# The first loads of a fused attention and SwiGLU kernel put on one DMA queue, with one dummy product fewer

## The chip, the cores and the metric

The kernel runs on one core of one Trainium2 chip. The metric is device time in microseconds (us), the median over several executions. With one core there is no other die to compare with; all runs quoted are of the state "fast". Different experiments ran on different chips, and each was timed in turn with the kernel before on its own chip. "Span" is the length of one profiled execution; it is about 1.7 us shorter than the device time of the same execution.

Engines in the profile: PE is the matrix engine (TensorE), PEld its weight loads, DVE the vector engine, ACT the scalar engine, POOL GpSimd, SP the sync engine, which here only issues loads and stores. SPq and ACTq are the sequencers of SP and ACT issuing a DMA. Queue q1 in the DMA view is the sync queue, q10 the scalar queue.

## The reference

The block mixes linear attention and a SwiGLU over the same x (2048 tokens of 512 values), with a gate per token:

```python
qkv = x @ wqkv                       # 32 heads of 16
phi = lambda t: where(t > 0, t + 1, exp(t)) + 1e-6
kv  = sum over tokens of phi(k) v;   z = sum over tokens of phi(k)
a   = (phi(q) @ kv) / (phi(q) . z + 1e-6) @ wo
b   = (silu(x @ w1) * (x @ w3)) @ w2
out = sigmoid(x . gate_w) * a + (1 - that) * b
```

All inputs are bf16. For this change only the start matters: k needs x transposed and wk, and phi(k) then multiplies x (the products called XP).

## The kernel before

Four loads of 256 KB come first. x tiles 0-1, wk's second half and x tiles 2-3 go by the sync queue, wk's first half by the scalar queue. Behind them on the sync queue come the remaining x tiles, once through a transposing load and once plainly.

```python
dq = nc.sync
dq.dma_start(out=x_sb[:, 0:2, :], in_=x_pairs[0])                       # x tiles 0-1
nc.scalar.dma_start(out=wk_sb[:, 0:2, :], in_=wqkv_r[:, 0:2, D:2*D])    # wk, first half
dq.dma_start(out=wk_sb[:, 2:4, :], in_=wqkv_r[:, 2:4, D:2*D])           # wk, second half
dq.dma_start(out=x_sb[:, 2:TPB, :], in_=x_pairs[1])                     # x tiles 2-3
...                                  # ACT: a one-element exp, which loads its table
for tb in range(1, NTB):
    dq.dma_start(out=xT[...], in_=x2d[...], transpose=True)
    dq.dma_start(out=x_sb[...], in_=x_r[...])
...                                  # all other weights
```

While these loads run PE has nothing to compute. It is given dummy products on constants, meant to have its clock up when work comes (in this trace dummies of 512 columns start 0.42 us apart, products of the same width from 5.5 us on 0.216):

```python
emit_warm(TB, TB, TB, TB, TB, TB, P, P, P)     # six of 512 columns, three of 128
...
emit_xT(0); emit_xT(1)               # PE transposes x tiles 0-1 (xTp), copies by DVE and ACT
for kc, t in ((0,0),(1,0),(0,1),(1,1),(2,0),(3,0)):
    emit_k_mm(k0[t], t, kc)          # kc 0-1 need wk's first half, kc 2-3 the second
emit_k_phi(k0[0], 0)
emit_xT(2); emit_xT(3)               # needs x tiles 2-3
...                                  # ten more key products, then XP and the rest
```

PE's order is fixed by hand, so a product that waits holds back the products behind it.

## Time and profile before

| | before |
|---|---|
| time, median of the first 3 runs | 180.62 us (180.34 to 180.81) |
| span of the profiled execution | 178.7 us |
| PE busy | 174.9 us, 98% |
| PE's first real instruction (xTp) | 3.91 us |
| first product XP | 8.93 us |

The page's first part says what bounds the kernel. Columns: engine, busy us, share of the span, instructions.

```profile
span 178.7 us, 2488 instructions
PE 174.9 (98%) x893; PEld 84.6 (47%) x893; DVE 118.2 (66%) x205; ACT 66.6 (37%) x126; POOL 61.4 (34%) x69
```

The chain of waits in the first 16 us (start, length, what) shows PE alone from 0.84 us on: dummies, transposes, key products, XP, with hardly a gap. (Where two groups of products overlap in the pipeline the chain lets the second start where the first ends, so its XP stands at 9.09; the timeline has the true start, 8.93.)

```profile
0.84 3.04 PE warm L161 x9
3.88 0.03 issue
3.91 1.03 PE xTp L174 x8
4.95 1.54 PE k L184 x6
6.48 0.45 PE xTp L174 x8
6.93 2.16 PE k L184 x10
9.09 0.86 PE XP L204 x4
```

The DMA view lists issues with KB and the time from issue to landing, here in three narrow windows: the issues at 0.80 (scalar) and 0.81 (sync), then wk's second half at 1.26, then x tiles 2-3 at 1.72.

```profile
wk_sb<-in_A_wqkv_dram ACTq DMA_DIRECT2D x1, 256.0 KB, 3.8
x_sb<-in_A_x_dram SPq DMA_DIRECT2D x1, 256.0 KB, 3.1
...
wk_sb<-in_A_wqkv_dram SPq DMA_DIRECT2D x1, 256.0 KB, 4.0
...
x_sb<-in_A_x_dram SPq DMA_DIRECT2D x1, 256.0 KB, 4.3
```

Adding issue and landing: x tiles 0-1 at 3.9, wk's halves at 4.6 and 5.3, x tiles 2-3 at 6.0 us. Each comes 0.04 to 0.63 us before PE uses it (3.91, 4.74, 5.89, 6.32). So the start is balanced closely, and PE waits for none of the last three.

### The profile page before, as it was taken

The numbers are of one execution on the slowest core, as the hardware profiler recorded it, in microseconds if no ns is written. First come the engines' busy times: TensorE is split into PE (matmuls) and PEld (weight loads), VectorE is DVE, ScalarE is ACT, GpSimd is POOL, SyncE is SP. The second block draws the span as 40 slices with busy tenths as digits, with TensorE's granted clock in tenths as the row PEclk, the third lists the DMA queues.
The fourth block names the chain that finished last, engine by engine and source line by source line (L and its number), as shares of the span: only waits on it lengthen the run. The fifth ranks groups of instructions, "written<-read, shape, count | busy, mean of one in ns | idle before, by whom it ended". The sixth has DMA issues, their size and how long they took to land.

```text
span 178.7 us, 2488 instructions
## 1 busy us (share of the span) xinstructions
PE 174.9 (98%) x893; PEld 84.6 (47%) x893; DVE 118.2 (66%) x205; ACT 66.6 (37%) x126; POOL 61.4 (34%) x69
## 2 busy tenths in 40 slices
PE   8999999999999999999999999999999999999993
PEld 3544444474444545444444544444545444444463
DVE  0588867696998837398786375978754669776000
ACT  3642322666533333342433333342433323341221
POOL 5187575646353323262003232620032328100000
PEclk9999999999999999999999999999999999999999
DMA  6999999601005010124000111240001023300011
GB/s 177 265 280 290 298 362 355 216 0 28 9 11 108 0 48 29 44 54 93 0 4 6 38 37 37 59 93 2 0 7 58 15 62 64 61 0 0 29 44 50
DMA packets 29085, 14.88 MB, mean 83 GB/s; under 512 B 19632, under 2 KB 28816, under 8 KB 29072
## 3 DMA queue, kind: packets, MB, share of 16 engines
q1 hardware_dynamic: 28800, 14.46, 29.5%
q10 hardware_dynamic: 272, 0.26, 0.5%
q8 instruction: 7, 0.11, 0.3%
q14 instruction: 6, 0.05, 0.1%
HBM read 8.42 MB, written 2.10 MB: 59 GB/s over the span
## 4 chain that ended last, share of the span: by engine, by line
PE 98%; DVE 0%; issue 0%; DVEq 0%
PE o_ps L355 19%; PE up_ps L318 19%; PE gate_ps L310 19%; PE XP L204 8%; PE o_ps L346 8%; PE q_ps L217 8%; PE k_ps L184 6%; PE r_ps L241 3%; PE k L184 2%; PE o_ps L350 2%; PE warm L161 2%; PE xTp L174 1%; PE kvT_ps L413 1%; PE W_ps L440 0%; DVE o_out L364 0%; PE z_ps L431 0%
## 5 line engine op out<-in xcount | busy, mean ns | idle before, releaser
L318 PE MATMUL up_ps<-xT,w_sb 128*128 128x512 bf16 x160 | 41.1, 379 | 0.0
L310 PE MATMUL gate_ps<-xT,w_sb 128*128 128x512 bf16 x160 | 41.1, 379 | 0.0
L225 POOL TENSOR_TENSOR qz<-pq,z_sb 128x512 f32<-128x512 bf16 x16 | 18.5, 1164 | 60.3 <-DVE pq L145 58.4
L323 ACT ACTIVATE th<-gate_ps 128x512 bf16<-128x512 f32 x40 | 23.9, 597 | 38.1 <-PE gate_ps L310 37.7
L355 PE MATMUL o_ps<-w_sb,hT 128*128 128x512 bf16 (+2 forms) x180 | 37.5, 355 | 0.0
L325 DVE SCALAR_TENSOR_TENSOR gs<-th,gate_ps 128x512 bf16<-128x512 bf16 x40 | 27.4, 684 | 5.8 <-ACT th L323 5.5
L328 DVE TENSOR_TENSOR hT<-up_ps,gs 128x512 bf16<-128x512 f32 x40 | 27.6, 691 | 3.8
L142 DVE TENSOR_SCALAR phi_m<-phi_e 128x512 bf16<-128x512 bf16 x32 | 14.1, 440 | 19.8 <-ACT phi_e L140 19.7
L355 PEld LDWEIGHTS <-hT 128*128 128x128 bf16 x180 | 16.8, 98 | 17.9
L318 PEld LDWEIGHTS <-w_sb 128*128 128x128 bf16 x160 | 15.6, 98 | 18.9
L310 PEld LDWEIGHTS <-w_sb 128*128 128x128 bf16 x160 | 15.6, 98 | 18.7
L360 ACT ACTIVATE o_out<-o_ps,omg 128x512 bf16<-128x512 f32 (+2 forms) x17 | 11.2, 656 | 30.4 <-PE o_ps L355 30.4
L290 POOL TENSOR_TENSOR pqn<-pq,rden 128x512 bf16<-128x512 bf16 x16 | 16.6, 1056 | 14.0 <-DVE rden L283 11.7
L194 POOL TENSOR_TENSOR pks<-pks,pk_sb 128x512 f32<-128x512 f32 x15 | 17.3, 1155 | 8.3 <-DVE pk_sb L145 7.8
L228 DVE TENSOR_REDUCE den<-qz 128x32 f32<-128x512 f32 x16 | 11.0, 685 | 9.0 <-POOL qz L225 8.9
L346 PE MATMUL o_ps<-W_sb,pqT 128*128 128x512 bf16 (+2 forms) x72 | 16.8, 355 | 0.0
L217 PE MATMUL q_ps<-wq_sb,xT 128*128 128x512 bf16 x64 | 16.3, 379 | 0.0
L204 PE MATMUL XP<-pk_sb,x_sb 128*128 128x512 bf16 x64 | 16.2, 379 | 0.0
L140 ACT ACTIVATE phi_e<-k_ps 128x512 bf16<-128x512 f32 x12 | 7.2, 597 | 15.4 <-PE k_ps L184 13.1
L184 PE MATMUL k_ps<-wk_sb,xT 128*128 128x512 bf16 x48 | 12.3, 379 | 0.0
L140 ACT ACTIVATE phi_e<-q_ps 128x512 bf16<-128x512 f32 x16 | 9.6, 597 | 7.0 <-PE q_ps L217 5.8
L145 DVE SCALAR_TENSOR_TENSOR pq<-q_ps,phi_m 128x512 bf16<-128x512 f32 x16 | 11.1, 691 | 0.5
(59 smaller groups left out, 119.3 us busy)
## 6 DMA issues: line engine op xcount, KB each, us to landing
w_sb<-in_B_w_dram SPq DMA_DIRECT2D x6, 640.0 KB, 8.6
out_dram<-o_out SPq DMA_DIRECT2D x15, 128.0 KB, 1.7
x_sb<-in_A_x_dram SPq DMA_DIRECT2D x3, 512.0 KB, 4.0
x_sb<-in_A_x_dram SPq DMA_DIRECT2D x2, 256.0 KB, 3.7
wq_sb<-in_A_wqkv_dram SPq DMA_DIRECT2D x1, 512.0 KB, 5.1
wv_sb<-in_A_wqkv_dram SPq DMA_DIRECT2D x1, 512.0 KB, 6.8
wo_sb<-in_A_wo_dram SPq DMA_DIRECT2D x1, 512.0 KB, 10.0
wk_sb<-in_A_wqkv_dram ACTq DMA_DIRECT2D x1, 256.0 KB, 3.8
```

The costliest lines, as they stand in the source:

```text
L184: nc.tensor.matmul(k_ps[:], lhsT=xT[:, kc, t * P : (t + 1) * P], rhs=wk_sb[:, kc, :], start=(kc == 0), stop=(kc == KC - 1),)
L194: nc.gpsimd.tensor_add(pks[:], pks[:], pk_sb[:, t, :])
L204: nc.tensor.matmul(XP_ps[dc][:], lhsT=x_sb[:, t, dc * P : (dc + 1) * P], rhs=pk_sb[:, t, :], start=(t == 0), stop=(t == NT - 1),)
L217: nc.tensor.matmul(q_ps[:], lhsT=xT[:, kc, ts_tok], rhs=wq_sb[:, kc, :], start=(kc == 0), stop=(kc == KC - 1),)
L225: nc.gpsimd.tensor_tensor(out=qz[:], in0=st[tb, "pq"][:, tt, :], in1=z_sb[:], op=ALU.mult)
L310: nc.tensor.matmul(gate_ps[:], lhsT=w1_sb[:, kc, fsl], rhs=xT[:, kc, tok_sl], start=(kc == 0), stop=(kc == KC - 1),)
L318: nc.tensor.matmul(up_ps[:], lhsT=w3_sb[:, kc, fsl], rhs=xT[:, kc, tok_sl], start=(kc == 0), stop=(kc == KC - 1),)
L323: nc.scalar.activation(out=th[:], in_=gate_ps[:], func=ACT.Tanh, scale=0.5)
L325: nc.vector.scalar_tensor_tensor(out=gs[:], in0=th[:], scalar=1.0, in1=gate_ps[:], op0=ALU.add, op1=ALU.mult)
L328: nc.vector.tensor_tensor(out=st[tb, "hT"][:, fc, :], in0=up_ps[:], in1=gs[:], op=ALU.mult)
L346: nc.tensor.matmul(o_ps[:], lhsT=st[tb, "pqT"][:, c, tsl], rhs=W_sb[:, c, a:b], start=(c == 0), stop=False,)
L355: nc.tensor.matmul(o_ps[:], lhsT=st[tb, "hT"][:, fc, tsl], rhs=w2_sb[:, fc, a:b], start=False, stop=(fc == FC - 1),)
```

## The change

The intent: x tiles 0-1 should not share the DMA engines with wk's first half (in the kernel before, from 2.8 to 3.0 us, 26 packets of the one ran beside 20 of the other), so that they land sooner; then one dummy product can go, and PE begins real work about 0.43 us earlier. The whole diff:

```diff
     dq.dma_start(out=x_sb[:, 0:2, :], in_=x_pairs[0])
-    nc.scalar.dma_start(out=wk_sb[:, 0:2, :], in_=wqkv_r[:, 0:2, D : 2 * D])
+    dq.dma_start(out=wk_sb[:, 0:2, :], in_=wqkv_r[:, 0:2, D : 2 * D])
     dq.dma_start(out=wk_sb[:, 2:4, :], in_=wqkv_r[:, 2:4, D : 2 * D])
     dq.dma_start(out=x_sb[:, 2:TPB, :], in_=x_pairs[1])
@@
-    emit_warm(TB, TB, TB, TB, TB, TB, P, P, P)
+    emit_warm(TB, TB, TB, TB, TB, P, P, P)
```

## The prediction

> **What bounds it now.** TensorE. The page gives PE 174.9 us of a 178.7 us span (98%), and the chain of waits is PE in 98% of it. So time can only be won before the first product that counts, or after the last. At the start the chain reads: issue to 0.84 us; nine dummy products (warm) 0.84 to 3.88; the transposes of x tiles 0-1 (xTp) from 3.91; then key products. From 3.91 on PE is hardly idle. The list of waits shows one stop that a load causes: xTp's weight loads wait 0.3 us for DMA x_sb, issued at 0.81 and landed 3.1 us later, at about 3.9. So dummies and first x load end together; neither is worth shortening alone.
>
> **The load.** In narrow windows of the DMA view the first x load's packets (sync queue) start near 1.75 us. Packets of wk's first half (scalar queue) appear from 2.6 us on, when about 70 of x's 128 packets have run, and take a third to a half of the engines until x is through, near 3.3. [...] With wk behind x on one queue, x's last 60 packets should run at about the 369 GB/s that both got together: 0.33 us instead of 0.7. x then lands near 3.45 (estimate), 0.45 earlier.
>
> **The cost.** One more issue on SP, about 0.45 us, so wk's second half, x tiles 2-3 and the transposing loads are issued that much later. wk's first half landed at 4.6, its first product began at 4.74; wk's second half 5.26, first product 5.89; x tiles 2-3 6.0, transposes 6.32. The engines are saturated from 2.6 us on and the order of bytes hardly changes, so I expect these landings to stay or come slightly earlier. The first transposing load should land near 8.1 and is used at 9.8.
>
> **The dummies.** Cold 512-column products start 0.42 us apart (six from 0.84 to 2.93); hot ones 0.216 us. Dropping one lets PE reach the transposes at about 3.3, x at 3.45: xTp starts about 0.43 us earlier.
>
> **How much is kept.** The hot spacing begins at about 5.1 us[...]. So 0.43 us more of useful work is done at half speed, worth about 0.22 us hot. Small waits for copies in this stretch (0.28 us for a DVE copy) move with it, so some of the rest may be kept. Gain 0.2 to 0.35 us of 180.6, near the spread of the three runs (180.34 to 180.81).
>
> **Predicted: 180.35 us**, 8 in 10 between 180.0 and 180.7. Faster by over 2%: 0.005; within 2%: 0.99; slower by over 2%: 0.005.
>
> **What would show it.** Eight dummies ending near 3.45; first x load landing in about 2.6 us; xTp starting at 3.45 to 3.5; first key product near 4.3; the first product XP (before at 8.93) near 8.65, everything after shifted alike; no new PE wait for wk_sb or x_sb over 0.1 us.
>
> **What would make it wrong.** wk's first half lands later than 4.3 and the first key product waits; x tiles 2-3 land later than 6.0 and their transposes wait; x's landing does not move (PE idles where the dummy was, gain nil); or the clock turns hot later.

180.6 less the gain of 0.2 to 0.35 gives 180.25 to 180.4 us, and 180.35 was named. The 0.22 us is the estimate from this trace, 0.43 us at 0.42 us per product against 0.216; that the start of the hot spacing would stay where it was, on which it rests, was assumed and not shown.

## The result and the profile after

| | before | after |
|---|---|---|
| time, median of 6 runs | 180.47 us (180.28 to 180.81) | 181.43 us (181.08 to 181.53) |
| ratio | | 1.0049, 95% interval 1.0036 to 1.0062 |
| span | 178.7 us | 179.7 us |
| first product XP | 8.93 us | 9.78 us |

A ratio here is the mean time of one kernel's fast runs over that of the other's of the same rounds, so it is not quite the ratio of the medians. The changed kernel is 0.5% slower; it was forecast 0.1 to 0.2% faster, and 181.43 lies outside the range of 180.0 to 180.7. It is within the 2% called "same".

The page's first part of the changed kernel: PE is busy 1.3 us less in a span that is 1.0 us longer. (Some product records are missing from this trace, so the difference of busy times is rough.)

```profile
span 179.7 us, 2470 instructions
PE 173.6 (97%) x876; PEld 84.2 (47%) x892; DVE 117.6 (65%) x205; ACT 66.8 (37%) x126; POOL 61.3 (34%) x69
```

Its chain of waits no longer runs over the dummies. It runs over the sync queue's issues into the fourth load, x tiles 2-3, issued at 2.22 and landed 4.90 us later:

```profile
0.80 0.39 SPq L83
...
1.26 0.41 SPq L84
...
1.72 0.46 SPq L85
...
2.22 4.90 DMA x_sb<-in_A_x_dram
7.12 0.05 issue
7.17 0.62 PE xTp L174 x8
7.79 2.16 PE k L184 x10
9.95 0.86 PE XP L204 x4
```

The list of PE's waits (who, for what, us in total, times, longest) has only the start-up line for the kernel before within its first 14 us; the changed one has two more, for wk and for x:

```profile
PE k L184 <- DMA wk_sb<-in_A_wqkv_dram: 0.9, 1, 0.9
PE warm L161 <- PEq L473: 0.8, 1, 0.8
PE xTp L174 <- DMA x_sb<-in_A_x_dram: 0.4, 2, 0.2
```

The DMA view of the changed kernel for the four loads, issued at 0.80, 1.26, 1.72 and 2.22:

```profile
x_sb<-in_A_x_dram SPq DMA_DIRECT2D x1, 256.0 KB, 2.8
...
wk_sb<-in_A_wqkv_dram SPq DMA_DIRECT2D x1, 256.0 KB, 3.0
...
wk_sb<-in_A_wqkv_dram SPq DMA_DIRECT2D x1, 256.0 KB, 4.6
...
x_sb<-in_A_x_dram SPq DMA_DIRECT2D x1, 256.0 KB, 4.9
```

The first two loads land earlier than before (3.6 against 3.9, 4.3 against 4.6 us). The last two land 1.1 us later (6.3 against 5.3, 7.1 against 6.0). That they are issued 0.46 to 0.50 us later can explain less than half of it at most: the time from issue to landing itself grew by 0.6 us.

The windows view shows the hole. Columns: window, its length, busy us and instructions of PE, PEld, DVE, ACT and POOL, PE clock, DMA share, GB/s. (The DMA share counts overlapping packets and can pass 1, and the clock column says 1.00 here also where the clock was low, since the trace's clock record begins later; only the last column is used.) Before:

```profile
2.60:3.60 1.00, 1.00 (x6) 0.45 (x4) 0.00 (x0) 0.17 (x1) 0.40 (x1) 1.00 1.03 330
3.60:4.60 1.00, 0.97 (x10) 0.70 (x9) 0.25 (x1) 0.04 (x1) 0.00 (x0) 1.00 1.07 368
4.60:5.20 0.60, 0.60 (x6) 0.31 (x4) 0.33 (x2) 0.56 (x2) 0.00 (x0) 1.00 1.05 334
5.20:6.80 1.60, 1.60 (x15) 0.99 (x14) 0.17 (x1) 0.45 (x2) 0.00 (x0) 1.00 1.25 262
```

After:

```profile
2.60:3.60 1.00, 0.85 (x5) 0.31 (x3) 0.00 (x0) 0.00 (x0) 0.39 (x1) 1.00 1.05 383
3.60:4.60 1.00, 0.98 (x9) 0.84 (x10) 0.45 (x2) 0.33 (x2) 0.00 (x0) 1.00 0.87 163
4.60:5.20 0.60, 0.60 (x4) 0.26 (x3) 0.13 (x1) 0.34 (x2) 0.00 (x0) 1.00 0.86 238
5.20:6.80 1.60, 0.66 (x4) 0.10 (x1) 0.00 (x0) 0.00 (x0) 0.00 (x0) 1.00 1.08 234
```

For the first two loads the lone queue is as fast (383 against 330 GB/s here; later profiles have 306 and 318 on a lone queue, in e1 and h1, and 346 and 369 on two, in e2 and e6). From 3.6 us, about where the third load begins (0.49 MB had been moved by 3.6 us and 0.52, the size of two loads, by 3.7), the rate falls to 163 GB/s against 368. Over the 3.2 us from 3.6 to 6.8, the mean of the last three lines weighted by their lengths is 212 GB/s after and 309 before.

The packets themselves are no slower. From 4.0 to 4.4 us the trace has 58 packets of 1 KB after and 139 before, and the median one takes 46 ns in both (five of the 58 took over 100 ns, none of the 139). What differs is how many run, and which loads they belong to. The loads can be told by their packets: 1 KB for wk, 2 KB for x tiles 0-3, 256 B for the transposing load behind them. From 5.2 to 5.4 us, before:

```profile
DMA packets 149, 0.07 MB, mean 332 GB/s; under 512 B 133, under 2 KB 133, under 8 KB 149
```

After:

```profile
DMA packets 71, 0.06 MB, mean 280 GB/s; under 512 B 33, under 2 KB 62, under 8 KB 71
```

Before, wk is done (no packet from 512 B to 2 KB), and 16 packets of x tiles 2-3 run beside the transposing load. After, 29 packets of wk's second half (62 − 33) run side by side with 9 of x tiles 2-3 and some 30 of the transposing load: three loads of one queue that were issued one after the other.

**Where the 0.85 us at XP come from.** PE reaches the transposes of x tiles 0-1 0.29 us earlier (3.62 against 3.91). After four key products it stands until wk's second half is there: the fourth begins at 5.06 and would be followed 0.22 us later, but the fifth begins at 6.38, so 1.10 us are lost. After the sixth, at 6.60, the next transposes could begin near 6.81 and begin at 7.17: 0.36 us. Against that stand 0.32 us which the execution before spent between 3.91 and 6.32 and this one did not: 0.27 at its first two key products, which started 0.43 and 0.29 us after one another, and 0.05 at the transposes. (The clock record turns full at 5.31 us before and at 4.23 after; what sets it is not shown, see the section on the clock, and it does not move XP, since XP here follows the landing of x tiles 2-3.) 1.10 + 0.36 − 0.29 − 0.32 = 0.85. Later the shift neither grows nor shrinks by much: the last product ends at 175.81 before and 176.60 after, 0.79 us apart. The remaining 0.2 us of the two spans lie after that product, where the last store ends the span. That part (2.89 us before, 3.08 after) lies between 2.88 and 3.28 us in all eighteen profiles, with long and short ones among the kernels on one queue, so it is not shown to belong to the change.

### The profile page after: what moved, and what is told of

Its sections match the earlier page's. It is cut to its first block, busy times and chain, and to the rows that moved or that the text cites. A ratio compares the mean times of both kernels' runs of the same rounds, so it can differ in the third digit from the quotient of the medians.

```text
span 179.7 us, 2470 instructions
## 1 busy us (share of the span) xinstructions
PE 173.6 (97%) x876; PEld 84.2 (47%) x892; DVE 117.6 (65%) x205; ACT 66.8 (37%) x126; POOL 61.3 (34%) x69
## 4 chain that ended last, share of the span: by engine, by line
PE 94%; DMA 3%; SPq 1%; issue 1%; DVE 0%; DVEq 0%
PE o_ps L355 19%; PE gate_ps L310 19%; PE up_ps L318 19%; PE q_ps L217 8%; PE o_ps L346 8%; PE XP L204 8%; PE k_ps L184 6%; PE r_ps L241 3%; DMA x_sb<-in_A_x_dram 3%; PE o_ps L350 2%; PE k L184 1%; PE kvT_ps L413 0%; PE W_ps L440 0%; PE xTp L174 0%; SPq L85 0%
## 5 line engine op out<-in xcount | busy, mean ns | idle before, releaser
L318 PE MATMUL up_ps<-xT,w_sb 128*128 128x512 bf16 x156 | 40.5, 379 | 0.2
L142 DVE TENSOR_SCALAR phi_m<-phi_e 128x512 bf16<-128x512 bf16 x32 | 13.3, 416 | 20.4 <-ACT phi_e L140 20.3
```

The source lines that it names most:

```text
L318: nc.tensor.matmul(up_ps[:], lhsT=w3_sb[:, kc, fsl], rhs=xT[:, kc, tok_sl], start=(kc == 0), stop=(kc == KC - 1),)
```

## The experiments

Fifteen kernels were run, one of them twice (e7 and e7b). All but one give the right result; one is wrong. The measure beside the time is when a load has landed. In the trace each of these loads has 16 increments, and in the changed kernel the products that wait for x tiles 0-1, wk's second half and x tiles 2-3 begin at 3.62, 6.38 and 7.17 us, 0.04 to 0.05 us after the last one (3.58, 6.34 and 7.12). So the last one is taken as the landing; below stands its time, from one profiled execution of each kernel. The columns are x tiles 0-1, wk's two halves, x tiles 2-3, the first product XP, and the ratio to the kernel before of the same rounds.

| run | x 0-1 | wk 1st | wk 2nd | x 2-3 | XP | ratio (95% interval) |
|---|---|---|---|---|---|---|
| before | 3.87 | 4.56 | 5.26 | 6.03 | 8.93 | |
| after | 3.58 | 4.25 | 6.34 | 7.12 | 9.78 | 1.0049 (1.0036 to 1.0062) |
| e1_queue_only | 3.52 | 4.24 | 6.34 | 7.03 | 9.69 | 1.0061 (1.0041 to 1.0081) |
| e2_dummy_only | 3.53 | 4.17 | 5.08 | 5.83 | 8.92 | 1.0019 (0.9988 to 1.0049) |
| e3_transpose_second | 3.59 | 4.26 | 6.17 | 6.84 | 9.50 | 1.0080 (1.0057 to 1.0103) |
| e4_tiny_scalar_load | 3.51 | 4.28 | 6.42 | 7.09 | 9.76 | 1.0049 (1.0025 to 1.0073) |
| e5_wk_in_one | 3.68 | 5.18 | 5.18 | 6.45 | 11.12 | 1.0048 (1.0004 to 1.0092) |
| e6_later_issue | 3.69 | 4.23 | 5.31 | 6.05 | 8.71 | 0.9999 (0.9979 to 1.0018) |
| e7_wk_second_half_scalar | 4.44 | 5.86 | 5.11 | 6.58 | 11.25 | 1.0029 (0.9976 to 1.0081) |
| e7b_repeat | 4.52 | 5.91 | 5.19 | 6.63 | 11.19 | 1.0085 (1.0026 to 1.0145) |
| e8_two_and_two | 3.91 | 4.47 | 6.06 | 6.23 | 9.63 | 1.0006 (0.9986 to 1.0026) |
| f5_x_first_scalar | 3.87 | 4.35 | 5.12 | 5.85 | 8.52 | 0.9997 (0.9969 to 1.0026) |
| f6_x_second_scalar | 4.25 | 4.97 | 6.16 | 4.04 | 9.23 | 1.0027 (1.0000 to 1.0053) |
| g2_wk_scalar_x_sync | 3.93 | 4.86 | 6.31 | 5.55 | 9.39 | 1.0023 (1.0003 to 1.0043) |
| h1_all_on_scalar | 3.45 | 4.09 | 6.39 | 7.16 | 9.82 | 1.0045 (1.0029 to 1.0060) |
| h2_two_kb_packets | 3.49 | 4.10 | 6.66 | 7.39 | 10.05 | 1.0034 (1.0005 to 1.0064) |
| h3_halves_exchanged | 3.63 | 6.91 | 4.29 | 7.69 | 10.85 | 1.0140 (1.0090 to 1.0190) |
| h4_wk_in_four | 3.43 | 5.21 | 5.89 | 6.66 | 9.32 | 1.0042 (1.0023 to 1.0060) |

### Which half of the change it is: e1 and e2

e1 is the changed kernel with the sixth dummy put back; e2 is the kernel before with the dummy taken away.

```diff
# e1, against the changed kernel
-    emit_warm(TB, TB, TB, TB, TB, P, P, P)
+    emit_warm(TB, TB, TB, TB, TB, TB, P, P, P)
# e2, against the kernel before
-    emit_warm(TB, TB, TB, TB, TB, TB, P, P, P)
+    emit_warm(TB, TB, TB, TB, TB, P, P, P)
```

Expected of e1:

> The queue change alone, with all six 512-column dummies kept. Theory A (wk's second half and x tiles 2-3 land about 1.1 us later with one queue; the dummy plays no part in the loss): landings of wk's second half near 6.3 and of x tiles 2-3 near 7.1 us as in the changed kernel, PE waits for both, time 181.3 to 181.5 us, because PE has caught up with the loads whatever the dummies do. Rival (the missing dummy lets PE run ahead into the loads, or changes the clock): time back at 180.4 to 180.7. It also repeats the landings once.

Expected of e2:

> The shorter dummies alone, wk's first half still on the scalar queue. Theory A: x tiles 0-1 land at about 3.9 us as before, PE idles about 0.4 us for them where the dummy was, the rest is as before: 180.3 to 180.6 us, no loss. Rival (the missing dummy is the loss): 181.0 to 181.4 us.

e1 took 181.37 us (the kernel before 180.24 in the same rounds), with landings at 6.34 and 7.03. e2 took 180.41 us, with landings at 5.08 and 5.83. So the queue alone gives the whole loss. (e2 missed its expectation that x tiles 0-1 land near 3.9; they landed at 3.53.) The hole in the transfers is there in e1 too, only spread otherwise, and deepest late:

```profile
3.60:4.60 1.00, 1.00 (x12) 0.99 (x11) 0.34 (x2) 0.26 (x1) 0.00 (x0) 1.00 0.98 278
4.60:5.20 0.60, 0.60 (x4) 0.22 (x2) 0.24 (x1) 0.50 (x2) 0.00 (x0) 1.00 0.89 328
5.20:6.80 1.60, 1.34 (x5) 0.34 (x3) 0.00 (x0) 0.00 (x0) 0.00 (x0) 1.00 1.11 135
```

Their weighted mean is 216 GB/s, as in the changed kernel (212). In e1 the lateness is that of a few increments: thirteen of the 16 increments of wk's second half came by 5.07 us, the last three at 6.00, 6.23 and 6.34. The missing dummy neither costs nor gains anything that this interval could show (0.2 us of gain to 0.9 us of loss): e2's transposes begin 0.34 us earlier than those of the kernel before (3.57), yet XP begins at 8.92 against 8.93. In e2's trace the PE clock record turns full at 5.65 us, before at 5.31, so e2 did its extra early work at the low clock. e2's x tiles 0-1 also landed at 3.53, though wk's first half went by the scalar queue beside them as before: the 3.87 of the first profile, from which the prediction worked, is the late end of what this load does on two queues (3.53 to 3.87 in before, e2 and e6). The lone queue's 3.43 to 3.63 (without e5) is earlier than these by much less than the predicted 0.45, and e2 has the same without a lone queue. wk's first half gains as little: 4.09 to 4.28 on a lone queue (e5 and h4, which cut wk otherwise, and h3, which exchanges the halves, left out), 4.17 and 4.23 in e2 and e6.

### Rivals close at hand: e3 and e4

The change also moved two other things: the transposing load stands right behind four loads of one queue, and ACT, no longer issuing a load, starts its table load at 0.80 instead of 1.27 us.

```diff
# e3, against the changed kernel (for tb == 1 only)
-    dq.dma_start(out=xT[...tb 1...], in_=..., transpose=True)
-    dq.dma_start(out=x_sb[...tb 1...], in_=...)
+    dq.dma_start(out=x_sb[...tb 1...], in_=...)
+    dq.dma_start(out=xT[...tb 1...], in_=..., transpose=True)
# e4, against the changed kernel
+    tiny = consts.tile([1, D], BF16, name="tiny")
+    nc.scalar.dma_start(out=tiny[:], in_=gate_w.rearrange("(o d) -> o d", o=1))
```

Expected of e3:

> The changed kernel, but the first transposing load is issued after the x tiles 4-7 load instead of before it. Theory B (the transposing load's many small packets on the same queue slow what was issued just ahead of it): wk's second half lands near 5.3 and x tiles 2-3 near 6.1 us. Rival theory A (a lone queue gets less out of the engines here, whatever follows): they land near 6.3 and 7.1 as in the changed kernel. The time itself is not the measure, since the transposed tiles may come too late for the key products of tile 4 (up to 1 us more).

Expected of e4:

> The changed kernel plus a 1 KB load of gate_w, unused, issued first on the scalar queue, so the scalar engine's table load starts at about 1.27 us as before instead of 0.80. Theory C (the moved table load disturbs the loads): landings near 5.3 and 6.0, time 180.2 to 180.6 us. Theory A (what counts is that one of the big loads goes by the second queue): landings near 6.3 and 7.1, time 181.3 to 181.5.

Neither brought the landings back: 6.17 and 6.84 in e3, 6.42 and 7.09 in e4 (181.26 us). So the table load is out. The transposing load behind may account for the 0.2 to 0.3 us that e3 came earlier, no more. (e3's time, 181.70, also holds the later transposed tiles.)

### Later issue or lone queue: e6

With two queues, a 1 KB load put into the sync queue delays the issue of wk's second half and of x tiles 2-3 to 1.62 and 2.08 us (1.72 and 2.22 in the changed kernel):

```diff
# e6, against the kernel before
     nc.scalar.dma_start(out=wk_sb[:, 0:2, :], in_=wqkv_r[:, 0:2, D : 2 * D])
+    tiny = consts.tile([1, D], BF16, name="tiny")
+    dq.dma_start(out=tiny[:], in_=gate_w.rearrange("(o d) -> o d", o=1))
     dq.dma_start(out=wk_sb[:, 2:4, :], in_=wqkv_r[:, 2:4, D : 2 * D])
```

Expected of e6:

> The kernel before (wk's first half on the scalar queue, all dummies), with a 1 KB unused load put into the sync queue after x tiles 0-1, so wk's second half and x tiles 2-3 are issued about 0.46 us later, as in the changed kernel. Theory A (the lone queue is the cause): landings near 5.3 and 6.1 us, time 180.2 to 180.6. Rival theory D (the later issue is the cause): landings near 6.3 and 7.1, time 181.1 to 181.5.

It took 180.72 us, equal to the kernel before in the same rounds (180.72), with landings at 5.31 and 6.05. A later issue of 0.36 us, three quarters of that in the changed kernel (0.46 to 0.50), costs nothing, as the prediction had said. The windows view of e6:

```profile
2.60:3.60 1.00, 1.00 (x6) 0.45 (x4) 0.00 (x0) 0.17 (x1) 0.39 (x1) 1.00 1.06 369
3.60:4.60 1.00, 0.95 (x12) 0.56 (x11) 0.51 (x2) 0.43 (x2) 0.00 (x0) 1.00 1.04 325
4.60:5.20 0.60, 0.60 (x4) 0.29 (x3) 0.00 (x0) 0.23 (x1) 0.00 (x0) 1.00 1.03 356
5.20:6.80 1.60, 1.45 (x14) 0.69 (x12) 0.39 (x2) 0.82 (x2) 0.00 (x0) 1.00 1.27 255
```

No hole: from 3.6 to 6.8 us the weighted mean is 296 GB/s, where the changed kernel moved 212.

### Is it the sync queue, or any lone queue: h1

All four loads go by the scalar queue. The sync queue's transposing load had to be held back by other means, or it would have come first; fills of its target on GpSimd hold it to 2.82 us.

```diff
# h1, against the kernel before
-    dq.dma_start(out=x_sb[:, 0:2, :], in_=x_pairs[0])
+    nc.scalar.dma_start(out=x_sb[:, 0:2, :], in_=x_pairs[0])
     (the same for wk's second half and x tiles 2-3)
+    for kc in range(3): nc.gpsimd.memset(xT[:, kc, TB : 2 * TB], 0.0)
+    (and a two-element fill of each later x and xT target; SP's order fixed by hand)
```

Expected of h1:

> All dummies; the four first loads all on the scalar queue in the changed kernel's order; the sync queue's first transposing load is held by fills of its target on GpSimd until about 3 us (2.7 in the changed kernel). Theory L (a lone queue, whichever): wk's second half near 6.3 and x tiles 2-3 near 7.0 us, time 181.1 to 181.6. Theory S (the sync queue with the transposing loads behind): near 5.3 and 6.2, time 180.3 to 180.9.

It took 181.10 us (the kernel before 180.44), with landings at 6.39 and 7.16, the same as on the sync queue. In the windows view the hole is there, with a weighted mean of 205 GB/s:

```profile
3.60:4.60 1.00, 1.00 (x12) 0.99 (x11) 0.34 (x2) 0.89 (x3) 0.96 (x3) 1.00 0.70 187
4.60:5.20 0.60, 0.60 (x4) 0.23 (x2) 0.25 (x1) 0.51 (x2) 0.00 (x0) 1.00 0.94 335
5.20:6.80 1.60, 1.46 (x5) 0.40 (x3) 0.00 (x0) 0.00 (x0) 0.00 (x0) 1.00 1.32 167
```

So it is not the sync queue, and not sharing a queue with the transposing loads (whose first packet runs at 5.16 us in h1, so that until then the scalar queue is alone). It is these four loads on one queue, whichever.

### Size of packets, place in memory, number of loads: h2, h3, h4 and e5

```diff
# h2, against e1: WRONG RESULT on purpose; wk filled from contiguous rows, 128 packets of 2 KB
+    wo_pairs = A_wo.rearrange("(g p j) n -> g p j n", p=P, j=2)
-    dq.dma_start(out=wk_sb[:, 0:2, :], in_=wqkv_r[:, 0:2, D : 2 * D])
+    dq.dma_start(out=wk_sb[:, 0:2, :], in_=wo_pairs[0])       # and the second half alike
# h3, against e1: wk's second half issued before its first
# h4, against e1: wk in four loads of 128 KB
# e5, against the changed kernel: wk in one load of 512 KB
-    dq.dma_start(out=wk_sb[:, 0:2, :], in_=wqkv_r[:, 0:2, D : 2 * D])
-    dq.dma_start(out=wk_sb[:, 2:4, :], in_=wqkv_r[:, 2:4, D : 2 * D])
+    dq.dma_start(out=wk_sb[:], in_=wqkv_r[:, :, D : 2 * D])
```

Expected of e5:

> All on the sync queue as in the changed kernel, but wk's two halves in one load of 512 KB. Theory A1 (a lone queue runs its engines dry where one of its loads ends and the next but one should start): with one boundary fewer the whole of wk lands near 5.3 and x tiles 2-3 near 6.2 us; PE waits about 0.9 us for the whole wk, then hardly for x: time 180.7 to 181.3. Theory A2 (a lone queue is slower per byte whatever its boundaries): wk near 6.3, x tiles 2-3 near 7.1, time 181.3 to 181.9.

Expected of h2:

> WRONG RESULT on purpose: all dummies, all four loads on the sync queue, but wk's halves filled from wo, whose rows are contiguous, so that each half is 128 packets of 2 KB instead of 256 of 1 KB, with the same bytes. Theory P (packets are the cause): second half near 5.2, x tiles 2-3 near 6.0 us, time 180.2 to 180.7. Rival (bytes or loads on a lone queue): near 6.3 and 7.0, time 181.1 to 181.6.

Expected of h3:

> All dummies, all four loads on the sync queue, wk's second half before its first. Theory L: the second of the four loads lands near 4.3, the third near 6.3, x tiles 2-3 near 7.0 us, whichever half is which. Theory R (the rows of wk's second half are slow to read): the second of the four loads lands at 5.0 or later, the third soon after. The time is 181.3 or more either way, as the first key products need the half that comes third.

Expected of h4:

> All dummies, all on the sync queue, wk in four loads of 128 KB. Theory N (each further load on the queue costs): the last quarter of wk after 6.4, x tiles 2-3 after 7.3 us, time 181.4 to 182.0. Theory L or P: about 6.3 and 7.1, as with two halves; time 181.1 to 181.6.

In h3 the load that comes second lands at 4.29 and the third at 6.91, although the halves have changed places: the third load is late, whichever half it is (by 0.6 us more than expected, and so is x tiles 2-3 at 7.69).

h4 missed its expectation in the other direction. With wk in four loads the last part landed at 5.89 and x tiles 2-3 at 6.66, between the good and the bad case. Here too it is the third load that is late: wk's first quarter landed at 3.77, the second only at 5.21, the others 0.34 us apart behind it. The rate is 132 GB/s from 3.6 to 4.6 us.

e5 has its third load only at the end: all of wk landed at 5.18, near A1's 5.3 and far from A2's 6.3, and x tiles 2-3 at 6.45, nearer A1's 6.2. So bytes as such are not slow on a lone queue. A1's reason, the boundaries between loads, is not borne out by this: h4 has more of them than e1 and lands earlier. e5's time has two kinds of execution: 181.03 and 181.06 us, in A1's range, and 182.49 and 182.81. The profiled one (182.81 us) stayed at the low clock until 9.34 us; in all of them PE must wait for the whole of wk.

h2 does not settle the number of packets. Its profiled execution has the lateness in full with half as many packets (6.66 and 7.39). But that is the slowest of its four (181.64 us); two others took 180.48 and 180.62 us, no more than the kernel before (180.44), and its median, 180.90, lies in neither expected range. So 2 KB packets do not prevent the lateness; whether they make it rarer is open.

Together: on a lone queue the first two loads land as early as on two, the third lands late, and the fourth follows it as closely as it does on two queues (0.78 us in the changed kernel, 0.77 in the kernel before). The third load is late because some of its 16 increments come far behind the others: they lie between 4.73 and 6.34 us in the changed kernel, between 4.69 and 5.26 before. Why these fall behind the runs do not show. That each increment stands for one of the page's 16 DMA engines would be a guess: the trace does not say which engine a packet ran on.

### Other divisions between two queues: e7, e7b, e8, f5, f6, g2

Is any use of the second queue good enough, and does one beat both kernels? All keep the six dummies and differ from the kernel before only in the queue of these four loads and, with it, their order of issue. One diff is shown; the others are told in a line each.

```diff
# f5: x tiles 0-1 on the scalar queue, all else on sync
-    dq.dma_start(out=x_sb[:, 0:2, :], ...)
-    nc.scalar.dma_start(out=wk_sb[:, 0:2, :], ...)
+    nc.scalar.dma_start(out=x_sb[:, 0:2, :], ...)
+    dq.dma_start(out=wk_sb[:, 0:2, :], ...)
# f6: x tiles 2-3 on scalar, all else on sync
# g2: both halves of wk on scalar, both x loads on sync
# e8: wk's first half and x tiles 2-3 on scalar, the other two on sync
# e7 and e7b (the same kernel twice): wk's second half on scalar, its first on sync
```

Expected of f5:

> All dummies; x tiles 0-1 alone on the scalar queue, wk's halves and x tiles 2-3 on the sync queue. Theory A, strict form (the other queue must still have packets left at about 3.6 to 4.2 us, when the sync queue changes over to its next load): the scalar queue is empty by 3.4 us, so wk's second half comes after 5.6 and x tiles 2-3 after 6.5 us, time 180.8 to 181.5. Theory A, loose form (any load taken off the sync queue is enough): near 5.2 and 6.0, time 180.2 to 180.7.

Expected of f6:

> All dummies; x tiles 2-3 on the scalar queue from the start, x tiles 0-1 and wk's halves on the sync queue. Theory A: the engines stay fed, all four loads landed by about 6.0 us, x tiles 2-3 first of the last two (near 4.6), wk's second half last (5.5 to 6.0): PE waits some 0.2 us for it; time 180.2 to 180.9. If the last of them lands at 6.5 or later, a second queue is not enough.

Expected of g2:

> All dummies; both halves of wk on the scalar queue, both x loads on the sync queue, two loads on each. Theory A: engines fed, x tiles 2-3 by 5.0 to 5.8, wk's second half by 5.3 to 5.8 us; time 180.2 to 180.8, no better than the kernel before by more than 0.2 us. Later than 6.3 for either would speak against theory A.

Expected of e8:

> The kernel before with x tiles 2-3 moved to the scalar queue behind wk's first half, so each queue has two loads; all dummies kept. Theory A: the engines stay fed, x tiles 2-3 land at 5.5 to 6.0 us, wk's second half at 5.3 to 5.6; time 180.0 to 180.5, at best 0.2 us under the kernel before, since PE there hardly waits for these loads. If it is over 180.9, feeding the engines is not the point.

Expected of e7:

> The kernel before with the halves of wk exchanged: the first half on the sync queue, the second half on the scalar queue; all dummies kept. Theory A (any second queue keeps the engines fed): all of wk by about 5.3 us (the halves together, so the first half later than 4.6), x tiles 2-3 near 6.0; time 180.3 to 180.9, any loss from the first half. Theory D or one that says wk's first half itself must go by the scalar queue: x tiles 2-3 near 7.0, time 181.2 or more.

Expected of e7b:

> The kernel with wk's halves exchanged between the queues once more, because the execution profiled of it was its one slow one (182.68 us against 180.5 to 180.9 of the others). Theory A: a usual execution has wk's halves by about 5.3 and x tiles 2-3 near 6.0 us, time 180.4 to 180.9. A second profile with x tiles 0-1 after 4.2 us would say that the slow start belongs to this order of loads.

f5 (180.37 us, the kernel before 180.40) is as good as the kernel before, landings 5.12 and 5.85, although its scalar queue is empty from 3.5 us on. That refutes the strict form of theory A: the second queue need not bridge the moment at which the third load starts; it is enough that one load is taken off the lone queue.

Do the engines stay fed in the others too? By the rate from 3.6 to 6.8 us, yes: all nine profiles with two queues (before, e2, e6, e7, e7b, e8, f5, f6, g2) moved 286 to 328 GB/s. The eight with four or more loads on a lone queue moved 198 to 245 (e5, with three, 285).

But a fed DMA is not enough; the order of the landings counts too. f6 had all four loads by 6.16 us, near its expected 6.0, but x tiles 2-3 came first (4.04) and wk's second half, which PE wants earlier, last. In g2 wk's second half was last too (6.31, just over the 6.3 that its expectation named as speaking against theory A). g2 took 180.87 us and f6 180.80 against 180.40; their intervals begin at 1.0003 and 1.0000. In e8 wk's second half came at 6.06 and x tiles 2-3 at 6.23, later than expected; its time, 180.78 us, missed the 180.0 to 180.5 forecast and equals that of the kernel before in the same rounds (180.72, ratio 1.0006).

e7 was the worst: x tiles 0-1, which run first, landed only at 4.44 and 4.52 us in its two profiled executions, where every other arrangement has them by 4.25; wk was complete only at 5.86 and 5.91. By e7b's own expectation this says that the slow start belongs to this order of loads, but both profiles are of long executions (182.68 and 182.61 us). The medians are 180.78 us in e7 and 181.99 in e7b (180.4 to 180.9 was expected), the single times 180.50 to 183.17. What the usual execution looks like, and why this order should disturb the x load, is open.

No arrangement beat the kernel before beyond the interval.

### The clock

e7b's profile shows what a low clock costs at the start. In the profile's view of one line, its key products up to 9.6 us (count, duration in ns minimum/median/maximum, first and last start) are nearly all slow:

```profile
L184 PE MATMUL k<-wk_sb,xT x9: 380/631/632, 5.9 to 9.5; 128*128 128x512 bf16 x9
```

and in the changed kernel, whose clock record is full from 4.23 us, none is:

```profile
L184 PE MATMUL k<-wk_sb,xT x16: 376/379/390, 4.4 to 9.6; 128*128 128x512 bf16 x16
```

In all eighteen profiles PE begins at 0.84 us, but where the trace has a clock record (fifteen of them) the clock turns full at times from 3.54 (e6) to 6.69 us (e8, with no wait of PE over 0.15 us to explain it), and in e5, e7 and e7b only at 8.7 to 9.3. In these three PE stood for 0.3 to 0.7 us before its first transposes, and their first key product began 0.7 to 0.8 us after the last of those transposes, against 0.27 us in e6. So with the same start of PE the clock turned full at times 3.15 us apart even without these three, and what sets the time is not shown. In all fifteen records the stretch at full clock lasts 170.67, 174.08 or 177.49 us, lengths that lie 3.41 us apart. Whether the pauses made the clock late in the three is not shown: no run varied them alone, and in h3, where PE stood for 2.2 us from 4.7 us on, the record still turns full at 5.37.

## Why the prediction was wrong

- **What bounds the start, and that x tiles 0-1 come just in time**: right. The chain of the changed kernel shows what happens when a load is late there: nearly all of what XP loses is still there at the end (0.85 us at XP, 0.79 us at the last product).
- **x tiles 0-1 land 0.45 us earlier without wk beside them**: the direction holds, the size does not. They landed at 3.58 instead of 3.45. On two queues the same load came between 3.53 and 3.87 (before, e2, e6); the first profile had its latest value.
- **Eight dummies end near 3.45, xTp at 3.45 to 3.5, first key product near 4.3**: 3.45, 3.62 and 4.41, so nearly right.
- **wk's first half no later than 4.3**: right, 4.25.
- **The later issue of 0.45 us is harmless**: right as far as tested: e6 has 0.36 us of it on two queues, with ratio 0.9999.
- **The step that failed**: "The engines are saturated from 2.6 us on and the order of bytes hardly changes, so I expect these landings to stay or come slightly earlier." In the kernel before, with two queues, the engines are saturated from 2.6 us on (DMA share 1.03 to 1.25 up to 6.8 us), and that was taken for a property of the loads. With one queue the rate from 3.6 to 6.8 us is 205 to 216 GB/s (changed kernel, e1, h1) against 296 to 309 (e6, before), and the last two loads land at 6.34 and 7.12 instead of 5.26 and 6.03. (The first transposing load, forecast for 8.1, landed at 8.97; its first use is at 10.64, so that cost nothing.) e1 and e2 show that this half of the change is the loss, h1 that it happens on either queue, e6 and f5 that one load on the other queue can remove it. What it is in the DMA that makes a lone queue's third load late stays open.
- **How the lateness becomes time**: in the kernels where x tiles 2-3 come last and hold PE, XP follows their landing by 2.66 us (7.12 to 9.78, and the same within 0.01 in e1, e3, e4, h1, h2 and h4). Before, XP followed by 2.90, so there were about 0.24 us of slack. The load came 1.09 us later; 1.09 − 0.24 = 0.85 us, what XP lost. The prediction named this lateness among the things that would make it wrong ("x tiles 2-3 land later than 6.0 and their transposes wait") but gave it no weight in its range.
- **The gain from the dummy, 0.2 to 0.35 us**: not seen. e2, the shorter dummies alone, shows no gain (ratio 1.0019, interval 0.9988 to 1.0049, so at most 0.2 us), and in the changed kernel PE waits for x tiles 2-3 whatever it did before.
- **The clock**: the prediction took the clock to turn full at about 5.1 us again. That was wrong: with PE beginning at 0.84 us as before it turned between 3.54 and 6.69 us, and later in three runs. It did not decide the result.

## What to carry to other kernels

When several loads are wanted at once at the start, do not judge a move to one queue by bytes and issue times alone: here four loads on a lone queue, and what followed them, moved some 210 GB/s where two queues moved some 300, and the third landed 1.1 us late with the fourth behind it. Look at each load's landing, not the first one's only, and keep beside it the slack of whoever waits (here 0.24 us). A landing read from one profile can be the latest of a spread (3.53 to 3.87 us here), so take it from two or three executions before planning on a few tenths of a us.
